# A fused state-space and bilinear feed-forward kernel: decay factors of later blocks by VectorE squares, and another order of the first pairs

## The chip, the cores and the metric

The kernel runs on one core of a Trainium2 chip. The time is device microseconds of one execution, given as the median of several executions. PE is the matrix engine (PEld its weight loads), DVE is VectorE, ACT is ScalarE, POOL is GpSimd and SP only issues transfers.

## The reference

Two layers follow each other. The first is a state-space scan over 768 tokens for 4 batches and 8 heads, the second a bilinear feed-forward layer over the 3072 tokens that come out:

```
for c in range(nc):                                   # chunks of the sequence
    cum = np.cumsum(log_a[chunk])                     # decay within the chunk
    M = (C B^T) * exp(cum_i - cum_j) * causal
    y[chunk] = M x + (C state) * exp(cum)
    state = exp(sum la) * state + sum_j B_j x_j exp(cum_last - cum_j)
x = y.transpose(0, 2, 1, 3).reshape(3072, 256)
out = ((x @ w_a) * (x @ w_b)) @ w_out                 # d_ff = 1536
```

Inputs and outputs are float32; the result of the chunked scan does not depend on the length of a chunk.

## The kernel before

**Blocks and pairs.** The kernel takes chunks of Q = 128 tokens, so there are NBLK = 6 blocks. A pair is two batches of one block; with NBP = 2 pairs a block there are 12 pairs, 0 to 11. Pairs 0 to 3 (p < P0, blocks 0 and 1) hold their tokens split by parity r (token 2i + r on partition i of a half); pairs 4 to 11 (blocks 2 to 5) hold one token a partition, and their B and C are turned by a DMA.

**Decay factors.** `scan` makes running products Pr[bh, block, q] of the decays, one row for each of the 32 (batch, head); `over_mid` makes rmid = 1 / Pr at the middle of each block. The factor of C is Pr times rmid, wanted with tokens on partitions: `factors_mm` gets it by a matmul of Pr with selr, a selection matrix scaled by rmid (`sel_over_mid`), and `factors` copies the result from PSUM into fC on ScalarE. fB is the reciprocal of fC (`fb`). Block 0 is done first, blocks 1 to 5 together.

**A pair's way.** `scale_bc` multiplies B and C with their factors, `transposes` turns them on PE and copies them to SBUF (B once for each parity of the head, through a column of the mask `par`, with the other heads set to zero; C once), `scores` makes C B^T of all heads in four PSUM banks SC[0..3], `mask` multiplies by the causal mask (on VectorE, or by a ScalarE copy and a GpSimd product with `by_pool`), `scale_x` makes the half-precision x, `pv` makes the output of the scan and the sums for the state, and copies the output into X2T (for pair 0 `pv_u` and `evac0` do so by halves of the channels).

**The feed-forward layer.** For pairs 0 to 3 a unit is `unit_mm` with Wa, `unit_mm` with Wb (four 256-column matmuls each, into one bank), a ScalarE copy of the first (`evac_a`) and a VectorE product (`times`). Then follow the matmuls with Wo (`out_mm`, `out_half`). For blocks 2 to 5 `bunit` and `bout` do the same for the four batches at once.

**Order.** The schedule is written out by hand: the order of the calls is the order of the instructions on each engine, and semaphores come from the data. Four PSUM banks are given out in turn by the string BANKS, one digit for each call of `bank`. Loads go by the queues of SP, ACT and POOL; the weights and the first loads of pairs 1 and 2 go by POOL, in order, behind POOL's own work. PE is filled with products of a zero tile (`warmup`) until the first weights are there.

The stretch that the change touches, as it is before, in the order of the calls: the four transposes of pair 1, two units with Wa, `scores(1)`, the third Wa unit, the factors of blocks 1 to 5, pair 1's masks, three Wb units, `pv(1)`, the products for the state factors G (gps), and then the units of pair 1.

Of the kernel before, what the change touches and what calls it, by code (L numbers as in the profile page):

```python
# [18 lines left out]
XS = 1024.0  # L19
YS = 16.0  # L20

BANKS = (
    "0123102310231012301230123012031230123013201320130213021302130213021320312031203102132013"
    "2013203102310231023103210321032103210321032103210231023102310231023102310231023102310231"
)


# [1 line left out]
def kernel(  # L29
# [13 lines left out]
    nc = tc.nc  # L43
# [52 lines left out]
    planes = [big.tile([128, 6, H * N], f16, name=f"planes{t}") for t in range(2)]  # L96
    causal_q = big.tile([128, Q], f16, name="causal_q")
    Pr = big.tile([BH, NBLK, Q], f32, name="Pr")
    rmid = big.tile([BH, NBLK], f32, name="rmid")
    selr = big.tile([BH, NBLK, 2, NBP * H], f32, name="selr")  # L100
    fB = big.tile([128, NBLK, 2, NBP, H], f32, name="fB")
# [25 lines left out]
    def bank(name):  # L127
        return psf.tile([128, 512], f32, name=name, tag=f"ff{next(banks)}")
# [58 lines left out]
    load1(nc.sync, 1, 0, 0)  # L187
    nc.sync.dma_start(c32, p32_t.ap())
    nc.vector.memset(warm.bitcast(u32), 0)
    nc.vector.memset(zero, 0.0)  # L190
    nc.gpsimd.memset(sel, 1.0)
    nc.gpsimd.affine_select(
# [5 lines left out]
        pattern=[[-H, 2], [-2 * H, NBP], [-1, H]],  # L198
        channel_multiplier=1,
    )  # L200
    nc.gpsimd.memset(ident, 1.0)
    nc.gpsimd.affine_select(
        out=ident, in_=ident, compare_op=ALU.is_equal, fill=0.0, base=0, pattern=[[-1, 128]], channel_multiplier=1
    )
    nc.gpsimd.memset(causal, 1.0)
    for bt in range(2):
        v = causal[64 * bt : 64 * bt + 64]
        nc.gpsimd.affine_select(  # L208
# [23 lines left out]
    def sel_over_mid(lo, hi, eng):  # L232
        eng.tensor_tensor(
            out=selr[:, lo:hi].rearrange("p k t c -> p k (t c)"),
            in0=sel.rearrange("p t b h -> p (t b h)").unsqueeze(1).broadcast_to((BH, hi - lo, 2 * NBP * H)),
            in1=rmid[:, lo:hi].unsqueeze(2).broadcast_to((BH, hi - lo, 2 * NBP * H)),
            op=ALU.mult,
        )

    def factors_mm(lo, hi, fps=None, k0=0):  # L240
        if fps is None:
            fps = bank("fps")
        w = 2 * NBP * H
        F = fps[:, k0 * w : (k0 + hi - lo) * w].rearrange("p (k r c) -> p k r c", k=hi - lo, r=2)
        for k in range(lo, hi):
            if k * NBP >= P0:
                for c0 in (0, 64):
                    nc.tensor.matmul(
                        F[c0 : c0 + 64, k - lo].rearrange("p r c -> p (r c)"),
                        Pr[:, k, c0 : c0 + 64],  # L250
                        selr[:, k].rearrange("p t c -> p (t c)"),
                        start=True,
                        stop=True,
                        skip_group_check=True,
                        tile_position=(0, c0),
                    )
                continue
            for r in range(2):
                for bt in range(2):
                    nc.tensor.matmul(  # L260
                        F[64 * bt : 64 * bt + 64, k - lo, r],
                        Pr[:, k].rearrange("p (i r) -> p r i", r=2)[:, r],
                        selr[:, k, bt],
                        start=True,
                        stop=True,
                        skip_group_check=True,
                        tile_position=(0, 64 * bt),
                    )
        return F.rearrange("p k r c -> p (k r c)")

    def factors(lo, hi, fps):
        factors_mm(lo, hi, fps)
        nc.scalar.copy(flat(fC, lo, hi), fps[:, 0 : (hi - lo) * 2 * NBP * H])

    def flat(f, lo, hi):
        return f[:, lo:hi].rearrange("p k r b h -> p (k r b h)")

# [4 lines left out]
    def scale_x(p, eng):  # L282
# [5 lines left out]
        else:  # L288
            eng.tensor_scalar(xo, xi, XS, None, ALU.mult)  # L289

    def scale_bc(p, which, eng, factor=None):
        blk, bp = divmod(p, NBP)
        name, f = (("bm", fB), ("cm", fC))[which]
        raw = by_token(pair_in[p][which]) if p >= P0 else pair_in[p][which].rearrange("p h r n -> p r h n")
        if p >= P0 and which:
            eng.tensor_tensor(  # L296
                out=planes[p % 2][:, 4:6].rearrange("p t (h n) -> p t h n", n=N),
                in0=raw,
                in1=f[:, blk, :, bp].unsqueeze(3).broadcast_to((128, 2, H, N)),
                op=ALU.mult,  # L300
            )
            return
        m_ = mid.tile([128, 2, H, N], f16, name=name, tag=name)
        eng.tensor_tensor(  # L304
            out=m_,
            in0=raw,
            in1=(f[:, blk, :, bp] if factor is None else factor).unsqueeze(3).broadcast_to((128, 2, H, N)),
            op=ALU.mult,
        )
        st.setdefault(p, {})[name] = m_  # L310
        if p >= P0:
            dst = planes[p % 2][:, 0:4].rearrange("p (t e) (m f n) -> p t e m f n", e=2, f=2, n=N)
            for e in range(2):
                eng.tensor_copy(dst[:, :, e, :, e], m_.rearrange("p t (m f) n -> p t m f n", f=2)[:, :, :, e])

    def transposes(p, ps=None, between=None, apart=False):
        s = st[p]
        if ps is None:
            ps = [SC[0], SC[1]] if apart else None
            on_dve = apart  # L320
        else:
            on_dve = True
        TB, TC = (TT[:, 0:256], TT[:, 256:512]) if ps is None else [t_.bitcast(f16)[:, 0:256] for t_ in ps]
        for T_, src in ((TB, s["bm"]), (TC, s["cm"])):
            for r in range(2):
                nc.tensor.transpose(
                    T_[:, r * 128 : (r + 1) * 128], src[:, r].rearrange("p h n -> p (h n)"), ident
                )
            if between:
                between()  # L330
                between = None
        BT = mid.tile([128, 2, 2, 2, 64], f16, name="bt", tag="bt")
        CT = mid.tile([128, 2, Q], f16, name="ct", tag="ct")
        b_ = []
# [261 lines left out]
    def unit_mm(p, k2, W):  # L596
# [13 lines left out]
                )  # L610
        return ps

    def evac_a(a_ps, on_dve=False):
        asb = ffh.tile([128, 512], f32, name="asb", tag="asb")
        (nc.vector.tensor_copy if on_dve else nc.scalar.copy)(asb, a_ps)  # L615
        return asb
# [123 lines left out]
    warmup(1, SC[3], 128)  # L740
    scale_bc(0, 0, nc.vector)
    scale_bc(0, 1, nc.vector, v.rearrange("p (r b h) -> p r b h", r=2, b=NBP)[:, :, 0])
    tb, tcp = bank("tb"), bank("tc")
    transposes(0, [tb, tcp], lambda: warmup(1, SC[3], 128))
    nc.scalar.copy(flat(fC, 0, 1), v)
    scan(3, 4)
    warmup(1, SC[3])
    warmup(2, SC[3], 128)
    scores(0)
# [14 lines left out]
    pv_u(0, 1, py, True)  # L764
    for bt in range(2):
        evac0(1, bt, (nc.scalar, nc.vector)[bt], py)
    scan(4, 5)
    w1 = load_w(1)
    for bt in range(2):
        load1(nc.gpsimd, 2, 0, bt)  # L770
    warmup(1, tcp, 128)
    transposes(1, apart=True)
    scan(5, NBLK)
    over_mid(1, NBLK)
    sel_over_mid(1, NBLK, nc.vector)
    aps = [unit_mm(0, 0, Wa), unit_mm(0, 1, Wa)]
    asb = [evac_a(aps[0])]
    nc.gpsimd.tensor_tensor(out=hr, in0=Pr[:, 0:NG, Q - 1], in1=rmid[:, 0:NG], op=ALU.mult)
    nc.gpsimd.tensor_tensor(out=hs, in0=hr, in1=Pr[:, 1:NBLK, 63], op=ALU.mult)
    nc.gpsimd.tensor_tensor(  # L780
# [2 lines left out]
        in1=selb.rearrange("p (b g) -> p b g", b=nb),  # L783
        op=ALU.mult,
    )
    scores(1)
    mask(product(1, 3), by_pool=True)
    aps.append(unit_mm(0, 2, Wa))
    asb.append(evac_a(aps[1]))
    asb.append(evac_a(aps[2]))  # L790
    fps = bank("fps")
    factors(1, NBLK, fps)
    scale_x(1, nc.scalar)
    for m in range(3):
        mask(product(1, m))
    bps = [unit_mm(0, k2, Wb) for k2 in range(3)]
    for bt in range(2):
        load1(nc.gpsimd, 2, 1, bt)
    load_wo(0)
# [9 lines left out]
    for c0 in (0, 64):  # L809
# [7 lines left out]
            tile_position=(0, c0),  # L817
        )
    nc.scalar.copy(G.rearrange("p b g -> p (b g)"), gps[:, 0 : nb * NG])
    for k2 in range(1, 3):  # L820
        times(0, k2, bps[k2], asb[k2])
    fb(1)
# [26 lines left out]
    h = unit(1, 5)  # L849
    scores(2)  # L850
    mask(product(2, 3), by_pool=True)
    mask(product(2, 0))
    mask(product(2, 1))
    mask(product(2, 2))
    h()
    scale_x(2, nc.scalar)
    scale_bc(3, 0, nc.gpsimd)
    scale_bc(3, 1, nc.gpsimd)
# [197 lines left out]
```

## Time and profile before

| | |
|---|---|
| median of 3 runs | 123.72 us (122.92 to 124.85) |
| the profiled execution | 122.51 us |
| its span, first to last instruction | 120.8 us |
| PE, DVE, ACT, POOL busy | 115.7, 85.2, 72.1, 62.3 us |
| TensorE clock granted | 0.999 |
| PE matmuls of the units, L601 and L667 | 27.8 and 57.1 us |
| transfers | 13.73 MB, mean 114 GB/s |

The page gives busy time for each engine, the chain of work that ended last, and groups of instructions by line. L601 is the matmul of `unit_mm`, L667 that of `bunit`, L248 and L260 those of `factors_mm`, L373 that of `scores` for the first pairs, L433 and L460 those of `pv_u` and `ds_mm`, L615 the copy of `evac_a`, L287 the ScalarE product of `scale_x`. A matmul of float32 operands appears as two records.

### The profile page before, as it was taken

The page shows a single profiled execution, that of the slowest core. Times are in us where ns is not written, and L with a number is a line of the kernel's source. Part 1 is how long each engine was busy: PE and PEld are TensorE (multiplying, and loading weights), DVE is VectorE, ACT ScalarE, POOL GpSimd, SP SyncE. Part 2 cuts the span into 40 slices and gives each one's busy share as a digit, 9 for nine tenths or more (in the row PEclk, how much of TensorE's full clock was granted, in tenths as well). Part 3 has the DMA queues.
Part 4 walks back from the last instruction along what each step waited for, and adds up shares of the span by engine and source line. Part 5 has one row for each costly group of instructions (what it writes and reads, how often), then busy time and mean ns, then how long its engine had stood idle before and what let it go on. Part 6 is the DMA issues. An engine that isn't in the chain of part 4 may idle for free.

```text
span 120.8 us, 3711 instructions
## 1 busy us (share of the span) xinstructions
PE 115.7 (96%) x1455; PEld 79.4 (66%) x1455; DVE 85.2 (71%) x162; ACT 72.1 (60%) x142; POOL 62.3 (52%) x108
## 2 busy tenths in 40 slices
PE   5889999999999999999999999999999999999990
PEld 2445889888898898644476464766464684555890
DVE  1887888882989898499984999677799445847100
ACT  0466757854965767877668637645646737566220
POOL 7999998972795676299731993138400000000200
PEclk9999999999999999999999999999999999999999
DMA  3999999986969999699998874869501012010032
GB/s 62 171 169 233 173 201 159 215 140 70 100 99 126 128 125 144 111 135 146 71 151 111 173 239 126 91 90 159 180 3 49 0 43 87 0 49 0 20 110 87
DMA packets 66641, 13.73 MB, mean 114 GB/s; under 512 B 61616, under 2 KB 66256, under 8 KB 66624
## 3 DMA queue, kind: packets, MB, share of 16 engines
q1 hardware_dynamic: 62448, 9.40, 50.7%
q0 software_dynamic: 2176, 3.74, 17.0%
q10 hardware_dynamic: 2000, 0.36, 1.6%
q8 instruction: 11, 0.18, 0.7%
q14 instruction: 6, 0.05, 0.1%
HBM read 11.13 MB, written 3.15 MB: 118 GB/s over the span
## 4 chain that ended last, share of the span: by engine, by line
PE 89%; DMA 4%; POOL 3%; issue 0%; ACT 0%; POOLq 0%
PE ops L694 18%; PE aps L667 18%; PE bps L667 17%; PE ops L637 9%; PE aps L601 9%; PE bps L601 9%; DMA Wa<-in_moe_w_a_dram 4%; PE SC L358 2%; PE SC L419 2%; POOL cn L148 1%; PE SC L373 1%; PE SC L433 1%; PE SC L508 1%; POOL bn L148 1%; POOL causal L208 1%; PE SC L460 1%
## 5 line engine op out<-in xcount | busy, mean ns | idle before, releaser
L615 ACT COPY asb<-aps 128x512 f32<-128x512 f32 x72 | 41.8, 586 | 14.1 <-PE aps L667 9.7
L679 DVE TENSOR_TENSOR hkb<-bps,asb 128x512 f16<-128x512 f32 x48 | 32.3, 687 | 12.8 <-ACT asb L615 11.6
L667 PE MATMUL aps<-XB,Wa 128*128 128x512 f16 x96 | 28.6, 379 | 0.0
L667 PE MATMUL bps<-XB,Wb 128*128 128x512 f16 x96 | 28.5, 379 | 0.0
L694 PE MATMUL ops<-Wo,hkb 128*128 128x256 f16 (+1 forms) x204 | 22.5, 267 | 0.0
L694 PEld LDWEIGHTS <-hkb 128*128 128x128 f16 x204 | 18.5, 98 | 3.1
L413 DVE TENSOR_TENSOR t<-SC,causal_q 128x512 f16<-128x512 f32 x27 | 17.1, 681 | 3.3 <-PE SC L358 3.3
L622 DVE TENSOR_TENSOR hk<-bps,asb 128x512 f16<-128x512 f32 x24 | 16.2, 685 | 2.4 <-ACT asb L615 1.2
L667 PEld LDWEIGHTS <-Wb 128*128 128x128 f16 x96 | 9.9, 103 | 10.9
L667 PEld LDWEIGHTS <-Wa 128*128 128x128 f16 x96 | 9.7, 103 | 9.1 <-issue 0.2
L708 POOL DMA_DIRECT2D out_dram<-osb x1 | 0.6, 639 | 27.3 <-ACT osb L706 27.3
L706 ACT ACTIVATE osb<-ops 128x256 f32<-128x256 f32 (+1 forms) x16 | 6.0, 376 | 14.3 <-PE ops L694 14.2
L601 PE MATMUL aps<-X2T,Wa 128*128 128x256 f16 x96 | 14.0, 273 | 0.1
L601 PE MATMUL bps<-X2T,Wb 128*128 128x256 f16 x96 | 13.8, 273 | 0.0
L637 PE MATMUL ops<-Wo,hk 128*128 128x256 f16 x96 | 11.5, 273 | 0.0
L601 PEld LDWEIGHTS <-Wa 128*128 128x128 f16 x96 | 9.5, 104 | 1.1 <-DMA Wa<-in_moe_w_a_dram 0.3
L601 PEld LDWEIGHTS <-Wb 128*128 128x128 f16 x96 | 9.8, 103 | 0.6
L411 POOL TENSOR_TENSOR t<-tmp,causal_q 128x512 f16<-128x512 f32 x5 | 5.8, 1159 | 8.0 <-ACT tmp L410 7.9
L637 PEld LDWEIGHTS <-hk 128*128 128x128 f16 x96 | 8.9, 98 | 1.4
L304 POOL TENSOR_TENSOR bm<-bn,fB 128x256 f16<-128x256 f32 x11 | 7.1, 641 | 4.8 <-DMA bn<-in_B_dram 3.6
L289 POOL TENSOR_SCALAR x<-xn 128x512 f16<-128x512 f32 x6 | 8.9, 1489 | 1.0 <-DMA xn<-in_x_dram 0.7
L296 POOL TENSOR_TENSOR planes<-cn,fC 128x256 f16<-128x256 f32 x8 | 5.0, 621 | 7.9 <-DMA cn<-in_C_dram 7.8
(95 smaller groups left out, 124.0 us busy)
## 6 DMA issues: line engine op xcount, KB each, us to landing
out_dram<-osb SPq DMA_DIRECT2D x22, 128.0 KB, 1.8
xn<-in_x_dram SPq DMA_DIRECT2D x7, 256.0 KB, 4.3
cn<-in_C_dram SPq DMA_DIRECT2D x8, 128.0 KB, 4.1
bn<-in_B_dram SPq DMA_DIRECT2D x8, 128.0 KB, 4.6
Wa<-in_moe_w_a_dram POOLq DMA_DIRECT2D x2, 384.0 KB, 5.9
Wb<-in_moe_w_b_dram POOLq DMA_DIRECT2D x2, 384.0 KB, 7.3
Wo<-in_moe_w_out_dram POOLq DMA_DIRECT2D x2, 384.0 KB, 7.2
xn<-in_x_dram POOLq DMA_DIRECT2D x4, 128.0 KB, 7.2
```

Of the source, the lines that this page charges most:

```text
L289: eng.tensor_scalar(xo, xi, XS, None, ALU.mult)
L304: eng.tensor_tensor(out=m_, in0=raw, in1=(f[:, blk, :, bp] if factor is None else factor).unsqueeze(3).broadcast_to((128, 2, H, N)), op=AL ...
L411: nc.gpsimd.tensor_tensor(out=o_, in0=tmp, in1=c_, op=ALU.mult)
L413: nc.vector.tensor_tensor(out=o_, in0=i_, in1=c_, op=ALU.mult)
L601: nc.tensor.matmul(ps[:, kk * 2 * Q : (kk + 1) * 2 * Q], W[k // 6][:, f, k % 6 // 3 * 384 : (k % 6 // 3 + 1) * 384].rearrange("p (c kk) -> ...
L615: (nc.vector.tensor_copy if on_dve else nc.scalar.copy)(asb, a_ps)
L622: nc.vector.tensor_tensor(out=s["hk"][:, 2 * k2 : 2 * k2 + 2, :].rearrange("p k q -> p (k q)"), in0=b_ps, in1=asb, op=ALU.mult)
L637: nc.tensor.matmul(o_ps[:, 0:d_model], hk[:, k, bt * Q : (bt + 1) * Q], Wo[:, k, :], start=(k == 0), stop=(k == NK - 1), skip_group_check= ...
L667: nc.tensor.matmul(t_, W[k // 6][:, f, k % 6 // 3 * 384 : (k % 6 // 3 + 1) * 384].rearrange("p (c kk) -> p kk c", kk=3)[:, k % 3], XB[:, b ...
L679: return lambda: nc.vector.tensor_tensor(out=s["hk"][:, k], in0=ps[1], in1=asb, op=ALU.mult)
L694: nc.tensor.matmul(o_ps[:, 0:w], hk[:, k, c * Q : (c + 1) * Q], Wo[:, k, cs], start=(k == 0), stop=(k == NK - 1), skip_group_check=True,)
L706: nc.scalar.activation(out=o_sb[:, 0:w], in_=o_ps[:, 0:w], func=AF.Copy, scale=1.0 / (YS * YS))
```

## The change

It has several parts, all but the last two in the first 16 us.

- The memsets of `ident` and `causal` go from GpSimd to VectorE.
- The scans of blocks 3 and 4 are called earlier, between the steps of pair 0.
- The first two Wa units of pair 0 are issued together (`units_mm`), first the two units' matmuls with channel half 0, then those with half 1.
- Pair 1's B is copied by one VectorE product with both parities (`joint`), its C by ScalarE.
- selr and the factor matmuls are made for block 1 alone.
- `scores(1)` and the mask product on GpSimd are called ahead of the three GpSimd products for hsx.
- Pair 1's x is scaled in two halves, by ScalarE (heads 0 to 3) and VectorE (heads 4 to 7), behind the masks.
- The third Wb unit of pair 0 is called behind gps instead of ahead of `pv(1)`.
- The factors of blocks 2 to 5 are made later, in pair 2's stretch: ScalarE multiplies Pr by rmid (`over_mid_late`), and VectorE transposes the result in squares of 32 x 32 (`turn_late`). They lie in fC in another order (`of_pair`).
- BANKS is another string.

```diff
+    Prm = big.tile([BH, NBLK, Q], f32, name="Prm")
...
     nc.vector.memset(warm.bitcast(u32), 0)
+    nc.vector.memset(ident, 1.0)
+    nc.vector.memset(causal, 1.0)
     nc.vector.memset(zero, 0.0)
...
-    nc.gpsimd.memset(ident, 1.0)
...
-    nc.gpsimd.memset(causal, 1.0)
...
         for k in range(lo, hi):
-            if k * NBP >= P0:
-                for c0 in (0, 64):
-                    nc.tensor.matmul(
...
-                continue
...
+    def over_mid_late(lo, hi):
+        for k in range(lo, hi):
+            nc.scalar.mul(Prm[:, k], Pr[:, k], rmid[:, k : k + 1])
+
+    def turn_late(lo, hi):
+        for c0 in range(0, Q, BH):
+            nc.vector.transpose(flat(fC, lo, hi)[c0 : c0 + BH].rearrange("p (k c) -> p k c", c=BH), Prm[:, lo:hi, c0 : c0 + BH])
+
+    def of_pair(f, blk, bp):
+        if blk * NBP >= P0:
+            return flat(f, blk, blk + 1).rearrange("p (b r h) -> p b r h", b=NBP, r=2)[:, bp]
+        return f[:, blk, :, bp]
...
+    def scale_x_split(p):
+        X16 = mid.tile([128, H, 2, D], f16, name="x16", tag="x16")
+        xi = pair_in[p][2]
+        st.setdefault(p, {})["X16"] = X16
+        for u in range(2):
+            o_, i_ = [t_[:, 4 * u : 4 * u + 4].rearrange("p h r d -> p (h r d)") for t_ in (X16, xi)]
+            if u:
+                nc.vector.tensor_scalar(o_, i_, XS, None, ALU.mult)
+            else:
+                nc.scalar.mul(o_, i_, XS)
...
+        if joint:
+            b_ = nc.vector.tensor_tensor(
+                out=BT.rearrange("p e r t i -> p e (r t i)"),
+                in0=TB.unsqueeze(1).broadcast_to((128, 2, 256)),
+                in1=par.unsqueeze(2).broadcast_to((128, 2, 256)),
+                op=ALU.mult,
+            )
+            c_ = nc.scalar.copy(
+                CT.rearrange("p t (i r) -> p r (t i)", r=2), TC.rearrange("p (r c) -> p r c", r=2)
+            )
...
+    def units_mm(p, ks, W, order):
+        pss = {k2: bank("aps" if W is Wa else "bps") for k2 in ks}
+        for k2, f in order:
+            for kk in range(2):
...
     scale_bc(0, 1, nc.vector, v.rearrange("p (r b h) -> p r b h", r=2, b=NBP)[:, :, 0])
+    scan(3, 4)
     tb, tcp = bank("tb"), bank("tc")
     transposes(0, [tb, tcp], lambda: warmup(1, SC[3], 128))
     nc.scalar.copy(flat(fC, 0, 1), v)
-    scan(3, 4)
+    scan(4, 5)
...
-    scan(4, 5)
...
-    transposes(1, apart=True)
+    transposes(1, apart=True, joint=True)
     scan(5, NBLK)
     over_mid(1, NBLK)
-    sel_over_mid(1, NBLK, nc.vector)
-    aps = [unit_mm(0, 0, Wa), unit_mm(0, 1, Wa)]
+    sel_over_mid(1, 2, nc.vector)
+    aps = units_mm(0, range(2), Wa, ((0, 0), (1, 0), (0, 1), (1, 1)))
     asb = [evac_a(aps[0])]
+    scores(1)
+    mask(product(1, 3), by_pool=True)
     nc.gpsimd.tensor_tensor(out=hr, in0=Pr[:, 0:NG, Q - 1], in1=rmid[:, 0:NG], op=ALU.mult)
...
-    scores(1)
-    mask(product(1, 3), by_pool=True)
...
-    factors(1, NBLK, fps)
-    scale_x(1, nc.scalar)
+    factors(1, 2, fps)
     for m in range(3):
         mask(product(1, m))
-    bps = [unit_mm(0, k2, Wb) for k2 in range(3)]
+    scale_x_split(1)
+    bps = [unit_mm(0, k2, Wb) for k2 in range(2)]
...
     nc.scalar.copy(G.rearrange("p b g -> p (b g)"), gps[:, 0 : nb * NG])
+    bps.append(unit_mm(0, 2, Wb))
...
     mask(product(2, 3), by_pool=True)
+    over_mid_late(2, NBLK)
     mask(product(2, 0))
     mask(product(2, 1))
     mask(product(2, 2))
     h()
+    turn_late(2, NBLK)
     scale_x(2, nc.scalar)
```

More of the change, by code (lines that the diff above doesn't have):

```diff
@@ L22 @@
 BANKS = (
-    "0123102310231012301230123012031230123013201320130213021302130213021320312031203102132013"
-    "2013203102310231023103210321032103210321032103210231023102310231023102310231023102310231"
+    "0123102310231032103210321032013210231021302130210321032103210321032130123012301203213021"
+    "3021301203120312031201320132013201320132013201320312031203120312031203120312031203120312"
 )
@@ L245, in factors_mm @@
         for k in range(lo, hi):
-            if k * NBP >= P0:
-                for c0 in (0, 64):
[L248 to L256, printed above, removed]
-                continue
             for r in range(2):
@@ L298, in scale_bc @@
                 in0=raw,
-                in1=f[:, blk, :, bp].unsqueeze(3).broadcast_to((128, 2, H, N)),
+                in1=of_pair(f, blk, bp).unsqueeze(3).broadcast_to((128, 2, H, N)),
                 op=ALU.mult,
@@ L306, in scale_bc @@
             in0=raw,
-            in1=(f[:, blk, :, bp] if factor is None else factor).unsqueeze(3).broadcast_to((128, 2, H, N)),
+            in1=(of_pair(f, blk, bp) if factor is None else factor).unsqueeze(3).broadcast_to((128, 2, H, N)),
             op=ALU.mult,
@@ L314, in scale_bc, with transposes @@
                 eng.tensor_copy(dst[:, :, e, :, e], m_.rearrange("p t (m f) n -> p t m f n", f=2)[:, :, :, e])
-    def transposes(p, ps=None, between=None, apart=False):
+    def transposes(p, ps=None, between=None, apart=False, joint=False):
         s = st[p]
@@ L333, in transposes @@
         CT = mid.tile([128, 2, Q], f16, name="ct", tag="ct")
+        if joint:
[8 more added lines that the diff above has]
+            )
+            tc.declare_no_dep(c_.ins, b_.ins.name, reason="reads of two banks")
+            s["BT"], s["CT"] = BT, CT
+            return
         b_ = []
@@ L611, in unit_mm @@
         return ps
+    def units_mm(p, ks, W, order):
+        pss = {k2: bank("aps" if W is Wa else "bps") for k2 in ks}
+        for k2, f in order:
+            for kk in range(2):
+                k = 2 * k2 + kk
+                nc.tensor.matmul(
+                    pss[k2][:, kk * 2 * Q : (kk + 1) * 2 * Q],
+                    W[k // 6][:, f, k % 6 // 3 * 384 : (k % 6 // 3 + 1) * 384].rearrange("p (c kk) -> p kk c", kk=3)[
+                        :, k % 3
+                    ],
+                    X2T[:, p, :, f],
+                    start=(f == 0 and kk == 0),
+                    stop=(f == 1),
+                    skip_group_check=True,
+                )
+        return [pss[k2] for k2 in ks]
     def evac_a(a_ps, on_dve=False):
```

## The prediction

> **What bounds the kernel now.** I read the page first: PE is busy for 96% of the span and holds 89% of the chain that ended last, with the weights' first load (4%) and POOL (3%) in front. Then the chain itself, for 10 to 17 us:
>
> ```profile
> 5.11 5.43 DMA Wa<-in_moe_w_a_dram
> 10.58 1.06 PE aps L601 x8
> 11.64 0.36 PE SC L373 x32
> 12.00 0.55 PE aps L601 x4
> 12.55 0.34 PE fps L260 x8
> 12.90 0.48 PE fps L248 x16
> 13.38 1.43 PE bps L601 x12
> 14.80 0.35 PE SC L433 x32
> 15.33 0.28 PE SC L460 x24
> 15.62 0.22 PE gps L810 x4
> 15.84 0.55 PE aps L601 x4
> 16.39 0.44 PE bps L601 x4
> ```
>
> Columns are start, length, what. Wa lands at 5.11 + 5.43 = 10.54, and from 10.58 the chain is PE without a break, to 118 us. Three kinds of saving are possible: an earlier 10.58, less PE work behind it, and neither counts if PE then waits for something else. A unit of four 256-wide matmuls is 0.44 here, 0.55 when it follows small ones. I compare the end of the first unit after gps: 15.84 + 0.55 = 16.39 us. Everything behind it has the same PE work in both kernels.
>
> What stands ready beside PE is in the timeline (start, length, engine, line, operation, tiles):
>
> ```profile
> 12.13 0.58 ACT L410 COPY tmp<-SC 128x512 f32<-128x512 f32 x1 [0.30 <-PE SC L373]
> 12.61 1.08 ACT L615 COPY asb<-aps 128x512 f32<-128x512 f32 x2
> 13.56 0.33 ACT L273 COPY fC<-fps 128x160 f32<-128x160 f32 x1
> 14.03 0.63 ACT L287 ACTIVATE x<-xn 128x512 f16<-128x512 f32 x1
> ```
>
> ```profile
> 9.17 0.82 POOL L304 TENSOR_TENSOR bm<-bn,fB 128x256 f16<-128x256 f32 x1
> 12.78 0.25 POOL L778 TENSOR_TENSOR hr<-Pr,rmid 32x5 f32<-32x5 f32 x1
> 13.55 1.16 POOL L411 TENSOR_TENSOR t<-tmp,causal 128x512 f16<-128x512 f32 x1
> 7.25 0.74 POOL L148 DMA_DIRECT2D xn<-in_x_dram  x1
> ```
>
> The last row is the issue of the second half of pair 1's x; the DMA view of that window gives it 6.7 us to landing, so 13.95. ACT scales x at 14.03, right behind the landing, ends at 14.66, and PE uses it at 14.80. So the x of pair 1 is only 0.1 us from being the bound already.
>
> **The change, part by part.**
>
> Memsets. On POOL ident's takes 0.20 and causal's 0.31. On VectorE a memset of 256 elements takes 0.27 (warm) and one of 128 0.17 (zero), so ident is ready at 1.19 + 0.17 = 1.36 and causal at 1.63; VectorE's next work waits for a_sb until 3.07, which hides this. POOL selects ident 1.37 to 1.66 and causal 1.66 to 2.47 (0.29, 2 x 0.40) and issues its first load at 2.49 instead of 2.88: 0.39 earlier, and so the seven loads behind it (cn twice, Wa, Wb, xn twice; bn first). Bounds on the landings: 0 (transfers already limit) and 0.39 (issue limits). In the view by windows the DMA share is 0.86, 0.94, 0.74, 0.91, 0.92, 0.89 for 2.5 to 5.5 us, and 1.10 and 1.14 for 8 to 10: against 1.12 some (1.12 - 0.88) / 1.12 x 3.0 = 0.64 us of transfer lay free, enough for 0.39, but shared with SP's and ACT's loads. I take 0.25: Wa 10.29, xn 13.70.
>
> Scans. The fourth and fifth (0.40 each) go into VectorE's idle 5.85 to 6.23 and 6.97 to 7.30; pair 0's C copy moves by 0.04, and the scores still wait for ACT's B (6.74). Cost nothing; uncovered it would be 0.4.
>
> PE's start. Pair 1's bm ends on POOL some 0.13 earlier, since the mask ahead of it waits for tmp (7.87) and no longer for the load issue (7.99). Its four transposes then end at 10.32 (10.45 before). Units start at max(10.29 + 0.04, 10.32) = 10.34, by 0.24 earlier.
>
> Order by channel half. The same eight matmuls. The halves of X2T are ready at 9.44 and 10.25, both ahead of 10.34: nothing gained. The first tile closes with the sixth matmul, so its ACT copy ends at 11.78; ACT's next, tmp, begins at 11.89. Hidden, by 0.1.
>
> B in one product. Two ACT passes (0.84) become one VectorE product of 512 elements: nearest rows 1.89 / 3 = 0.63 (mask) and 0.69 (hk); I take 0.69, bounds 0.63 and 0.84. C goes to ACT (0.43 on VectorE, 0.42 a pass on ACT). B is ready at 11.04, scores can start at 10.34 + 1.06 = 11.40: no wait. VectorE's stretch up to the masks was 10.50 to 11.78, 1.28; now 1.28 - 0.43 + 0.69 - 0.13 (the smaller selr) = 1.41, to 11.76. Masks begin 0.13 after the scores' end, 11.89: covered by 0.13.
>
> Factors. 0.48 of PE goes, and ACT's fC copy falls from 0.33 to 0.18 (the 128x32 copy). PE reaches pair 1's pv at 10.34 + 1.06 + 0.36 + 0.55 + 0.34 + (1.43 - 0.44) = 13.64, because the third Wb unit is put behind gps. Before, it was 14.80.
>
> What pv then waits for. ACT: tmp from 11.89, asb twice, fC: 11.89 + 0.58 + 1.08 + 0.18 = 13.73, just after the landing at 13.70. Half of x: SBUF 512 takes 0.63; PSUM rows of 512 and 256 give 0.59 and 0.38, so the half saves 0.20 and takes 0.43 (bounds 0.32, exactly half, and 0.43). It ends at 14.18, and PE follows 0.07 later as before: 14.25. VectorE: masks 11.89 to 13.78, its half 0.29 to 0.42 (the 128x128 and 128x256 X2T rows), to 14.20 at most, which the second half of pv needs at 14.43. So **PE stands from 13.64 to 14.25, 0.61**, where before it never stood. ScalarE's fixed price speaks against splitting: the Trainium skill's page "VectorE: DVE Perf Modes", section on the TRN2 errata, gives ScalarE 224 cycles plus one per element from SBUF, by an estimate 0.61 for 512 (row: 0.63, agreeing) and 0.40 for 256; with that the sum below would be 0.03 better.
>
> The sum: from 14.25, pv 0.35, state sums 0.46, gps 0.22, the moved unit 0.55, the first unit of pair 1 0.44 = 2.02, so 16.27 against 16.39: **0.1 us gained**. Of 0.24 (start) + 0.48 (factors) = 0.72, the stall takes 0.61 back.
>
> POOL's order. Its mask now comes first: loads end at 12.67, mask to 13.83, hr to hsx 0.80, to 14.63; gps needs it at 15.07. Hidden by 0.44.
>
> Banks. I followed each of the four banks through pair 3; the tile before is read at least 0.1 us before the next is written, so nothing. One missed costs a copy, 0.59.
>
> Late factors. Four ACT products of 32x128: between 0.28 (128x128 row) and 0.42, in all 1.1 to 1.7, from 25.12 where ACT has 1.10 idle; x of pair 2 ends 0 to 0.6 later, by 27.4, and pv needs it at 27.93. Four VectorE squares, which no row shows: between 0.17 (128-element memset) and 0.69 (512-element product), nearest 0.40 (32x128 scan), so 1.6 of the 1.64 that VectorE is idle there:
>
> ```profile
> 26.27 0.68 DVE L622 TENSOR_TENSOR hk<-bps,asb 128x512 f16<-128x512 f32 x1
> 28.59 0.42 DVE L493 TENSOR_SCALAR X2T<-SC 128x256 f16<-128x256 f32 x1 [1.64 <-PE SC L460]
> ```
>
> Cost nothing, at 0.69 each 2.76 - 1.64 = 1.1. The same page, section on the three transpose paths, has 311 ns for such a turn of 128x128 in bf16; by it the four would be 1.24, hidden; no run yet shows it. First use is POOL's cn of pair 4 at 30.14.
>
> **Against the runs.** The profiled execution took 122.51 (span 120.8 and 1.7 around it); less 0.1 it is 122.4. The median shown, 123.72, lies 1.2 above it, so I give 123.6 for a median. The three runs spread 122.92 to 124.85.
>
> **Rivals.**
>
> Forecast, x of pair 1 takes over as the bound: 123.6, own range 123.5 to 123.8. Chance 0.50.
>
> A, the loads come no earlier, transfers being saturated (share over 1 from 5.5 on speaks for it; the free 0.64 before it against). Units at 10.58, xn at 13.95, half of x 14.01 to 14.44, pv 14.51, the mark at 16.53: +0.14, 123.9. Chance 0.15.
>
> B, little stall: x is ready and pv waits only for the masks (13.78 + 0.06 = 13.84), the mark at 15.86: -0.5, 123.2. It needs x 0.4 sooner than the largest shift of the issue allows with ACT's chain as it is. Chance 0.10.
>
> C, slower: VectorE's half of x waits for POOL. In the row of 9.17 above POOL's bm takes 0.82, beside VectorE's cm (9.10 to 9.51), and 0.62 elsewhere: they hinder each other by 0.2. If the half, coming at 13.78, must wait for POOL's mask and hr to hsx (14.63), it ends at 15.05 and pv's second half starts 0.68 late: +0.6, 124.3. It decides from a start later than 13.95. The skill's "SBUF — State Buffer", section on who interferes with whom, says that one of the two blocks for a whole instruction; with the 0.82 row the trace agrees in sign. Between instructions VectorE can get in, so chance 0.15.
>
> D, the squares cost 0.7 or more: X2T of pair 2 is late by 1.1, 124.7; over 1.0 each it is 2.4 or more, 126. Chance 0.10, of it 0.05 for the upper end.
>
> That the factor matmuls stay is excluded by the code; only those of block 1 are left.
>
> **The numbers.** What a measurement can tell from no change is about 2%, 2.5 us. Only the top of D reaches it, and 0.03 of C with POOL's loads held up too: slower 0.08. No case gains 2.5; 0.04 is left for the spread of the medians. Within: 0.88. Range: from B less 0.8 of spread, 122.4, to D, 125.0.
>
> **What would show it.** Right: no L248 rows; Wa landing near 10.3; in the chain an ACT x or a DMA xn piece of some 0.6 just ahead of SC L433; the unit after gps ending near 16.3; ACT and VectorE rows at 25 to 28.6 with PE unbroken. Wrong: pv at 13.9 (B), a late DVE x row (C), a gap at 28.6 (D), or any PE gap behind 17 us.

## The result, and the profile after

The changed kernel takes 123.55 us, the median of 22 runs (122.94 to 124.57); the kernel before, in the same comparison, 123.3 us. The ratio is 1.0042 with a 95% interval of 1.0026 to 1.0059: slower by some 0.5 us, far inside the 2% named in the prediction, but with the sign opposite to the 0.1 us forecast. All ratios here leave out the slow executions of either kernel, so this one is not the quotient of the two medians, which lie only 0.25 us apart.

The profiled execution of after has a span of 122.2 us, 1.4 more than before's. This is its chain of waits (start, length, what), from POOL's sixth load to the first unit of pair 1:

```profile
6.22 0.66 POOL xn L149
6.88 8.14 DMA xn<-in_x_dram
...
15.11 0.42 ACT x L302
...
15.57 0.42 PE SC L459 x32
15.99 0.30 PE SC L486 x32
16.30 0.22 PE gps L853 x4
16.52 0.55 PE bps L627 x4
17.07 0.44 PE aps L627 x4
```

The line numbers have moved: L459 is pv (L433 before), L486 the state sums (L460), L853 gps (L810), L627 the units (L601). Before, the chain was PE from 10.58 on. Now it leaves PE at pv and runs through ScalarE's half of x into the load of x, as the prediction said it would: x has become the bound. But x landed at 15.02, not at 13.70. The point that the prediction followed, the end of pair 1's first unit, is 17.07 + 0.44 = 17.51, against 16.39 before and 16.27 forecast.

The same stretch in the timeline (start, length, engine, line, operation, tiles, and in brackets the engine's idle time ahead of the row and what ended it):

```profile
2.50 0.88 POOL L149 DMA_DIRECT2D bn<-in_B_dram  x1
5.77 0.42 DVE L317 TENSOR_TENSOR cm<-cn,fps 128x256 f16<-128x256 f32 x1 [0.17 <-DMA cn<-in_C_dram]
11.23 0.78 PEld L644 LDWEIGHTS <-Wa 128*128 128x128 f16 x8 [0.62 <-DMA Wa<-in_moe_w_a_dram]
15.12 0.35 DVE L300 TENSOR_SCALAR x<-xn 128x256 f16<-128x256 f32 x1 [0.43 <-DMA xn<-in_x_dram]
15.57 0.42 PE L459 MATMUL SC<-t,x 64*32 64x128 f16 x32 [1.02 <-ACT x L302]
```

POOL's first load is issued at 2.50, against 2.88 before, as worked out. Yet the first Wa matmul comes at 11.23 instead of 10.58, and VectorE waits for pair 0's C, which it did not do before. PE stands 1.02 us for x. The account of the 1.12 us at the first unit: units start 0.65 later; from there to pv 4.34 instead of 4.22 (0.48 of factors and 0.44 of a unit fewer, the 1.02 more); and from pv to the end of the unit 1.94 instead of 1.59, since the moved unit now lies there. The rest of the 1.4 is a second wait, far behind. Up to 77 us the chain of after runs 1.12 to 1.13 behind that of before (the same group of Wo matmuls at 77.69 and 76.56), and from the next such group on 1.35 (81.39 and 80.04). In between, PE waits for ScalarE's copy `osb`, which it does not do before:

```profile
79.98 0.05 issue
80.03 0.39 ACT osb L749
80.42 0.04 issue
80.46 0.59 PE bps L710 x2
```

By BANKS, this second `bps` tile lies in both kernels in the bank that `osb` empties, so the bank's order is not the difference. ScalarE comes late to `osb`, because its copies to XB have waited 0.48 for VectorE's state products U. VectorE starts these after 0.56 us of idle time instead of 0.18; the row names PE's state sums, but they had ended by 77.7, so why it starts late stays open:

```profile
76.74 0.97 DVE L565 SCALAR_TENSOR_TENSOR U<-SC,G,gU 128x64 f32<-128x64 f32 x4 [0.18 <-PE SC L447]
78.24 0.86 DVE L591 SCALAR_TENSOR_TENSOR U<-SC,G,gU 128x64 f32<-128x64 f32 x4 [0.56 <-PE SC L473]
```

One execution is not the median. The same kernel profiled again (r1 below) had a span of 121.1, 0.3 more than before's, with x at 13.76 and PE's stall at 0.37. Its first unit ends only 0.08 later than before's, and the other 0.22 is the same wait for `osb`, at 78.98. None of the other eighteen traces has a wait at that place. What differed between the two traces of the changed kernel was above all when the loads landed.

### The profile page after: what moved, and what is told of

Read it like the earlier page. It is cut to its first block, busy times and chain, and to the rows that moved or that the text cites. A ratio compares the mean times of both kernels' runs of the same rounds, so it can differ in the third digit from the quotient of the medians.

```text
span 122.2 us, 3688 instructions
## 1 busy us (share of the span) xinstructions
PE 115.8 (95%) x1439; PEld 79.1 (65%) x1439; DVE 87.6 (72%) x169; ACT 72.6 (59%) x145; POOL 62.0 (51%) x106
## 2 busy tenths in 40 slices
DMA packets 66641, 13.73 MB, mean 112 GB/s; under 512 B 61616, under 2 KB 66256, under 8 KB 66624
## 3 DMA queue, kind: packets, MB, share of 16 engines
HBM read 11.13 MB, written 3.15 MB: 117 GB/s over the span
## 4 chain that ended last, share of the span: by engine, by line
PE 85%; DMA 7%; POOL 4%; ACT 1%; issue 0%; DVE 0%; ACTq 0%
PE ops L737 18%; PE bps L710 17%; PE aps L710 17%; PE ops L680 9%; PE bps L627 8%; PE aps L627 8%; DMA xn<-in_x_dram 7%; PE SC L384 2%; PE SC L445 2%; POOL cn L149 1%; PE SC L459 1%; PE SC L534 1%; POOL bn L149 1%; POOL causal L209 1%; POOL Wa L166 1%; POOL Wb L166 1%
## 5 line engine op out<-in xcount | busy, mean ns | idle before, releaser
L665 DVE TENSOR_TENSOR hk<-bps,asb 128x512 f16<-128x512 f32 x24 | 16.3, 686 | 2.5 <-ACT asb L658 1.3
L710 PEld LDWEIGHTS <-Wa 128*128 128x128 f16 x96 | 9.7, 103 | 9.1 <-issue 0.2
L749 ACT ACTIVATE osb<-ops 128x256 f32<-128x256 f32 (+1 forms) x16 | 6.0, 377 | 14.2 <-PE ops L737 14.1
L627 PE MATMUL bps<-X2T,Wb 128*128 128x256 f16 x96 | 14.0, 273 | 0.0
L627 PE MATMUL aps<-X2T,Wa 128*128 128x256 f16 x88 | 12.9, 273 | 0.0
L627 PEld LDWEIGHTS <-Wb 128*128 128x128 f16 x96 | 9.7, 103 | 0.6
L627 PEld LDWEIGHTS <-Wa 128*128 128x128 f16 x88 | 8.8, 103 | 0.7
```

The costliest lines, as they stand in the source:

```text
L627: nc.tensor.matmul(ps[:, kk * 2 * Q : (kk + 1) * 2 * Q], W[k // 6][:, f, k % 6 // 3 * 384 : (k % 6 // 3 + 1) * 384].rearrange("p (c kk) -> ...
L665: nc.vector.tensor_tensor(out=s["hk"][:, 2 * k2 : 2 * k2 + 2, :].rearrange("p k q -> p (k q)"), in0=b_ps, in1=asb, op=ALU.mult)
L710: nc.tensor.matmul(t_, W[k // 6][:, f, k % 6 // 3 * 384 : (k % 6 // 3 + 1) * 384].rearrange("p (c kk) -> p kk c", kk=3)[:, k % 3], XB[:, b ...
L749: nc.scalar.activation(out=o_sb[:, 0:w], in_=o_ps[:, 0:w], func=AF.Copy, scale=1.0 / (YS * YS))
```

## The experiments

Every ratio is to the kernel before, on the same chip in the same call. Chips differ: the median of before was between 122.93 and 123.89 in five calls, so times of different calls are not compared directly. The intervals are some 0.3% wide on each side, about the size of what is looked for; the traces carry more of the argument than the ratios. They are compared up to the first unit behind gps, since ten of the twenty have PE waits between 35 and 68 us, of 0.05 to 1.6 us each, most of them for the turned B and C of the later blocks, in kernels with and without the change.

**The memsets, and with them the earlier loads.** e1 takes them out of the changed kernel, e2 puts them alone into the kernel before.

```diff
-    nc.vector.memset(ident, 1.0)        # e1; e2 is the reverse, in before
-    nc.vector.memset(causal, 1.0)
+    nc.gpsimd.memset(ident, 1.0)
+    nc.gpsimd.memset(causal, 1.0)
```

> The changed kernel with the two memsets back on GpSimd, all else as changed. Theory 1 (the earlier issue of POOL's loads makes them and pair 0's loads get in each other's way, so everything lands later): pair 0's C lands before 5.1 us again, Wa near 10.5, pair 1's x near 13.9 instead of 15.0; PE stands about 0.6 us ahead of pv instead of 1.0; 0.5 to 1.0 us faster than the changed kernel. Theory 2 (landings vary from one execution to the next, the memsets do nothing): landings anywhere between 10.5 and 11.2 for Wa, the time within 0.15 us of the changed kernel.

> The kernel before with the two memsets on VectorE, nothing else. Theory 1: Wa near 11.2, pair 1's x near 15.0, and with the third Wb unit still ahead of pv a stall of about 0.6 us there; 0.5 to 0.7 us slower than before. Theory 2: within 0.15 us of before, and POOL's first load issued at 2.5 instead of 2.9 us.

e1: 1.0026 (0.9999 to 1.0053). e2: 1.0042 (1.0016 to 1.0068), as much as the whole change. In e2 the loads are issued at 2.50, and the first Wa matmul is at 11.13 (10.37 in e1). To part the memsets from the earlier issue, e7 keeps e2 and lets POOL make two more memsets, on tiles that nobody reads, so that its first load goes out at 2.73:

```diff
+    nc.gpsimd.memset(ident_2, 1.0)
...
+    nc.gpsimd.memset(causal_2, 1.0)
```

> The kernel before with the two memsets on VectorE, as in the run with only the memsets, but GpSimd makes the same two memsets on spare tiles, so that its first load is issued at 2.9 us again. If the earlier issue costs the time: pair 0's C lands at 4.9 again instead of 5.1 to 5.7, the time is that of before within 0.2 us. If VectorE's memsets cost it (its later work or what GpSimd waits for): still 0.4 to 0.5 us slower than before.

e7: 1.0005 (0.997 to 1.0041). Three kernels were then run again on one chip, after as r1, e2 as r2 and e7 as r3:

> The changed kernel again, beside the next three on one chip, for its landings and its time: theory issue (the earlier first load of GpSimd makes pair 0's C land later and the start of PE with it) has C at 5.3 us or later, ratio 1.003 to 1.006; theory chance has C as in the kernels that issue at 2.9 us.

> The kernel before with only the memsets moved, again, on one chip with the next. Theory issue: pair 0's C 0.3 to 0.6 us later than in the next run, ratio to before 1.003 to 1.006. Theory chance: equal to the next within 0.2%.

> The memsets on VectorE with GpSimd's first load at 2.9 us, again, on one chip with the run ahead. Theory issue: ratio to before 0.999 to 1.001, C earlier than in the run ahead. Theory chance: no difference between the two.

r1: 1.0028 (1.0002 to 1.0054). r2: 1.0013 (0.9986 to 1.004). r3: 1.0005 (0.9982 to 1.0029). So the memsets in themselves cost nothing that shows. For the earlier issue the ratios lean one way (1.0042 and 1.0013 against 1.0005 twice) and overlap. The traces, those of the kernels below with the same warm-ups and loads included, lean the same way. In the five with the issue at 2.5 us (after, e2, e3, r1, r2) pair 0's last piece of C landed between 5.43 and 5.80 and the first Wa matmul came between 10.66 and 11.24, 11.0 in the mean. In the nine with the issue at 2.73 to 2.9 (before, e1, e4 to e8, r3, r4) it was 5.01 to 5.42 for C, without overlap, and 10.32 to 11.52, 10.7 in the mean, for the matmul. Pair 0's scores, which PE does first, began at 6.82 to 7.18 in the five and at 6.65 to 6.96 in the nine. The issue view of the first 2.7 us shows whom the early load meets (tiles, queue, count, size, us from issue to landing); first before:

```profile
cn<-in_C_dram SPq DMA_DIRECT2D x1, 32.0 KB, 2.8
cn<-in_C_dram ACTq DMA_DIRECT2D x1, 32.0 KB, 2.8
ch<-ph SPq DMA_DIRECT2D x1, 5.0 KB, 2.5
```

and after:

```profile
bn<-in_B_dram POOLq DMA_DIRECT2D x1, 64.0 KB, 3.8
cn<-in_C_dram SPq DMA_DIRECT2D x1, 32.0 KB, 3.3
cn<-in_C_dram ACTq DMA_DIRECT2D x1, 32.0 KB, 3.5
ch<-ph SPq DMA_DIRECT2D x1, 5.0 KB, 3.3
```

POOL's load of pair 1's B now runs beside the last small loads that pair 0 needs, on the queues of SP and ACT, and these take 0.5 to 0.8 us longer. They are needed first: C by VectorE (the wait of 0.17 in the timeline row of 5.77), ph by ScalarE's copy of B. The Trainium skill's page "DMA: Bandwidth & Descriptors", section "Issuing engines are not separate DMA queues", says that loads from several engines run on the same 16 DMA engines and interleave, so that another issuer saves only issue time; these rows agree, in that a load on one queue goes with longer loads on two others.

**The third Wb unit, and both parts undone.** e3 puts it back ahead of pv in the changed kernel; e6 is e3 and e1 together.

```diff
-    bps = [unit_mm(0, k2, Wb) for k2 in range(2)]
+    bps = [unit_mm(0, k2, Wb) for k2 in range(3)]
...
-    bps.append(unit_mm(0, 2, Wb))       # and BANKS to suit
```

> The changed kernel with the third Wb unit of pair 0 issued ahead of pv(1), as before the change, and the two bank digits swapped with it. If PE stands ahead of pv because pair 1's x is late (any reason), the unit fills 0.44 us of it: 0.4 to 0.5 us faster than the changed kernel, as fast as before or 0.1 faster. If instead pv's own order behind it sets the end (X2T late), no gain.

> The changed kernel with the memsets on GpSimd and the third Wb unit ahead of pv. Theory x: pv near 14.4 with no stall over 0.3 us, the first pair-1 unit ends near 16.0, 0.4 us ahead of the kernel before, ratio 0.9965. Theory fetch: a break in the state-sum matmuls to 15.4, the unit ends near 16.4, ratio 1.000.

e3: 1.0023 (0.9993 to 1.0052). e6: 1.0015 (0.9983 to 1.0048). What the unit's place is worth follows from rows. When x lands late, at L, the changed kernel starts pv at L + 0.55 (landing 15.02, pv 15.57) and ends the first unit 1.94 later: L + 2.49. Before, pv comes at L + 0.77 (e10 below: landing 14.95, pv 15.72), and the unit ends 1.59 later: L + 2.36. The halves of x gain 0.22, and the unit that filled the wait before costs 0.35. With the unit ahead again it is L + 0.55 + 1.65 (e3: pv 14.56, end 16.21) = L + 2.20. By these, an estimate, e6 should beat before by 0.16 where x binds; in its trace pv starts at L + 0.55, as it should, but the unit ends at L + 2.44, for the reason that follows.

**The late factors alone**, in the kernel before:

```diff
+    over_mid_late(2, NBLK)
...
+    turn_late(2, NBLK)                  # and factors(1, 2, fps) for factors(1, NBLK, fps)
```

> The kernel before with only the factors of blocks 2 to 5 made late (ScalarE products, VectorE squares, no factor matmuls for them). If pair 1's x sets pv in the kernel before as well, the 0.48 us of PE turn into a stall ahead of pv and the gain is 0 to 0.1 us. If PE alone bounds it, 0.45 us faster. If the squares are uncovered at 26 to 28.6 us, slower by what they exceed 1.64 us by.

e4: 1.0016 (0.9982 to 1.005). In this execution Wa landed 0.24 later than before's. From the first unit to pv it is 3.84 us instead of 4.22, so most of the 0.48 is gained there, and x, which landed at 13.89, costs PE only 0.04. Yet from pv (14.66) to the end of the unit (16.54) it is 1.88 instead of 1.59: PE stood 0.24 within the state sums, at 15.30.

**A break in the state sums.** e1's chain of waits shows the same break, for nothing that the profile names ("issue"):

```profile
13.91 0.42 ACT x L302
...
14.38 0.42 PE SC L459 x32
14.80 0.26 PE SC L486 x28
15.06 0.40 issue
15.46 0.21 PE SC L486 x4
15.67 0.22 PE gps L853 x4
```

e5 is e1 with x taken away as the bound:

```diff
-        xi = pair_in[p][2]
+        xi = pair_in[0][2]              # scale_x_split: pair 1 uses pair 0's x
```

> The changed kernel with the memsets on GpSimd (as in the run with them back), and pair 1's x scaled from pair 0's x tile, which has long landed: the output is another one, the instructions are the same. Theory x (the landing of pair 1's x alone sets pv): PE stands only for the masks, pv starts near 13.9 instead of 14.4, and the first pair-1 unit ends near 15.9 instead of 16.8: 0.5 to 0.9 us faster than with the memsets back. Theory fetch (PE also waits at its 450th record, in the state-sum matmuls, for a block of its own instructions, which has come 2.8 us after a transfer that starts near 12.6 in every trace): pv starts near 13.9, but the break moves to those matmuls and lasts until 15.4; the unit ends at 16.7, the time within 0.15 us.

e5: 1.0017 (0.999 to 1.0045). Its chain:

```profile
13.86 0.32 ACT x L302
...
14.22 0.47 PE SC L459 x32
14.69 0.24 PE SC L486 x28
14.92 0.53 issue
15.45 0.21 PE SC L486 x4
15.66 0.22 PE gps L853 x4
```

pv starts 0.16 earlier than in e1, the break grows by 0.13, and gps is at 15.66 against 15.67. Something other than x holds PE at that place in its program. Counted over its matmul and weight-load records, PE broke at the 447th or 448th in before, e1, e4, e5, e6, r3 and r4, with pauses of 0.2 or less there in e3, e7 and e8 too, and at the 446th in e10. In before it is the 0.09 here:

```profile
15.15 0.09 PE SC L460 x8
15.24 0.09 issue
15.33 0.28 PE SC L460 x24
```

The trace has beside it a transfer of the queue named "instruction", whose 11 transfers move 0.18 MB, 16 KB each: in these traces it starts at 12.4 to 13.1 us (15.39 in e10), and PE goes on 2.7 to 2.95 us after it starts (2.3 in e10). In the other nine traces PE comes to that record 2.86 to 4.0 us after the start, and shows no such pause. So PE seems to wait for its own next instructions, and these seem to be held up by the same loads as x; no view names the wait. With 36 records more ahead of it the place should move by 18 pairs of matmul and weight load; e8 is e6 with that, run again as r4:

```diff
-    warmup(6, SC[3])
+    warmup(24, SC[3], 128)
```

> As the run with the memsets back and the Wb unit ahead, with the first six 512-column warm-up matmuls cut into 24 of 128 columns: the same PE time, 36 more PE records ahead. Theory fetch: the block boundary and the start of its transfer move 36 records earlier in the program, into the scores and pv of pair 1; no break in the state sums, the first pair-1 unit ends near 16.0, 0.4 us faster than the same without it and 0.3 to 0.4 us faster than before. Theory x: no difference to the same without it, within 0.15 us.

> The version with memsets on GpSimd, the third Wb unit ahead of pv and 36 more PE records in the warm-up, on one chip with the changed kernel. All three causes (issue, order, fetch) are taken away in it: ratio to before 0.997 to 0.999, 0.5 us or more faster than the changed kernel, no break in the state sums. If the landing of pair 1's x is the only bound, 1.000.

e8: 1.0000 (0.9968 to 1.0031), with under 0.1 at that record; here Wa had landed late, at 11.47, and PE came to it late. r4: 1.0009 (0.9983 to 1.0036), and a break of 0.66 between the 6th and 7th state sum, where e6 has it (0.25) between the 24th and 25th: moved by 18, as the count says, but not gone.

Four kernels move it the other way or further. e9 is e6, and e10 is before, with the same twelve warm-up matmuls fewer; e12 is e6 with eighteen fewer; e11 is before with every wide warm-up cut in four, 90 records more.

```diff
-    warmup(6, SC[3])
-    warmup(2, SC[3], 128)
+    warmup(4, SC[3])
...
-    warmup(5, tcp)
+    warmup(3, tcp)                      # e9, e10; and six single ones of 128 columns
```

> The changed kernel with the memsets on GpSimd, the third Wb unit ahead of pv, and 12 warm-up matmuls fewer (all eight of 128 columns, two of the first six, two of the five behind pair 0's masks): 24 PE records fewer ahead. Theory fetch (PE can't pass its 447th record before about 15.4, whatever lies ahead): the 447th record now lies behind gps, no break in the state sums, the first pair-1 unit ends near 16.0, ratio to before 0.996 to 0.998. Theory x alone: as with the warm-ups, 1.000 to 1.0015.

> The kernel before with the same 12 warm-up matmuls left out. Theory fetch: its break in the state sums of 0.09 to 0.18 us goes, at most 0.2 us faster, ratio 0.998 to 1.000. Otherwise 1.000; slower if the granted clock falls without them.

> The kernel before with all its 512-column warm-up matmuls cut into four of 128: the same PE time, 90 PE records more ahead. Theory fetch: the 447th record lies 90 records earlier in the program, among pair 0's Wb units at about 14.1 us, and PE stands there until about 15.4: the first pair-1 unit ends 0.8 to 1.2 us later, ratio 1.006 to 1.010. Theory x alone: 1.000, since PE has the same work.

> As the run with 12 warm-up matmuls fewer, with 18 fewer in all (one left of the first six, none of the five): 36 PE records fewer. Theory fetch: no further gain than with 12 fewer, since x and the masks set pv, unless the clock falls for want of PE work ahead of 10 us, which would show as a granted clock below 1 there and 0.5 us or more lost.

e9: 1.002 (0.9987 to 1.0053), no break, but PE stood 0.51 for x, which landed at 14.49. e10: 1.0127 (1.0074 to 1.018). e11: 1.0087 (1.0053 to 1.0121), as expected from the break, but its trace does not show the break: the transfer starts at 11.69, and PE passes the record at 15.20. Where its time goes stays open. e12: 1.0104 (1.0057 to 1.0151); PE already stood 1.26 ahead of 8.61, and its matmuls then ran at about half the pace up to 14.2 (the eight Wa matmuls from 10.81 took 1.89, 1.05 in e9). In e9 and e10 pair 0's scores took 0.65 instead of 0.43, and the Wa matmuls 1.05 as ever. So leaving warm-ups out also slowed PE for a while, and changes more than the count. e10's chain of waits:

```profile
15.72 0.42 PE SC L433 x32
16.13 0.18 PE SC L460 x19
16.32 1.37 issue
17.69 0.25 PE SC L460 x13
```

Fewer records do move the break, from behind the 8th to behind the 19th state sum, but it became 1.37 long; here the instruction transfer started only at 15.39. What sets that start is open; moving records by warm-ups did not give a kernel without the wait.

**Less to transfer.** If both x and the instructions wait for the weights' transfer, a smaller one should free both. e13 is e6 with only the first half of Wb's first tile loaded and used twice; e14 is before with the same.

```diff
+                        W[0][:, :, 0:384], src.rearrange("(f p) e -> p f e", p=128)[:, :, 0:384]
...
+    def part3(W, k):
+        return 0 if W is Wb and k < 6 else k % 6 // 3 * 384
```

> The version with memsets on GpSimd and the third Wb unit ahead of pv, loading only the first half of Wb's first tile (192 KB less into SBUF ahead of pair 1's x) and using it twice: the output is another one, every engine's instructions are the same in number and size. Theory transfers (what the change saves on PE is eaten by waits for transfers: pair 1's x, and PE's own instruction block): x lands near 12.8, pv starts near 14.1 behind the masks and the Wb units, the first pair-1 unit ends near 15.7 if the instruction block comes earlier too, near 16.3 if it does not; ratio to before 0.994 to 0.996, or 0.999. Rival, the saving was never there (other waits on VectorE, ScalarE, GpSimd): 1.000 to 1.0015, as with the whole tile.

> The kernel before with the same half of Wb's first tile. Theory transfers: PE has work up to 14.8 anyway, so x near 12.8 gains nothing but the break of 0.1 us: ratio to before 0.998 to 1.000. If transfers bound the kernel before by more than that: below 0.998.

e13: 0.9969 (0.9949 to 0.9988), 122.53 us against 123.04. e14: 1.001 (0.9976 to 1.0043). e13's chain:

```profile
12.81 1.54 PE bps L637 x12
14.35 0.41 PE SC L469 x32
14.75 0.28 PE SC L496 x32
...
15.06 0.29 PE gps L863 x4
...
15.38 0.62 PE aps L637 x4
```

x lands at 12.99, the instruction transfer starts at 11.79 and there is no break; the unit ends at 16.00. In e14, with x at 12.98, it ends at 16.42, much as before (16.39). So the removed PE work shows as soon as x and the instructions are not late: of the 0.42 between the two ends, 0.38 is the shorter way from the first unit to pv (3.83 against 4.21) and 0.14 an earlier start of the units in that execution, less 0.10 behind pv. Which of the two, x or the instructions, held it back is not parted by this, and the intervals of the two ratios touch. e13 leaves out work that the layer needs and is no version to use. Of those that compute everything, none beat the kernel before; e8 comes nearest, at 1.0000 and 1.0009.

## Why the prediction was right or wrong

**Right: what would bind.** The factor matmuls of blocks 2 to 5 are gone, and the pieces of x stand in the chain right ahead of pv. In r1, where the loads landed almost as forecast (Wa 10.39, x 13.76), the chain of waits has the working almost term by term:

```profile
12.77 0.98 ACT asb L658 x2
...
13.84 0.43 ACT x L302
...
14.31 0.58 PE SC L459 x32
14.88 0.28 PE SC L486 x32
```

ScalarE's half at 13.84 (forecast 13.73), 0.43 long (0.43), pv at 14.31 (14.25), the unit's end at 16.47 (16.27). The last difference of 0.20 is 0.06 at pv's start, 0.05 in pv and state sums (0.86 for 0.81) and 0.09 at gps (15.17 to 15.48, 0.31 for 0.22).

**Wrong: the landings.** The step that failed is "I take 0.25: Wa 10.29, xn 13.70", with its bounds "0 ... and 0.39". The issue did come 0.38 earlier. The landings did not follow: over the five traces with the early issue and the nine with the later one, the median landing of Wa is 10.71 against 10.61, that of x 13.83 against 13.94. Where Wa did land early, in r1 at 10.39, the first matmul still came only at 10.66 (10.34 forecast); pair 0's scores, ahead of it on PE, had slipped to 7.11 from before's 6.73. So rival A, saturated transfers, was the nearer case, and it too had no change of the landings as its worst end. What could make the earlier issue a loss was not in the sum: the loads of SP and ACT that POOL's earlier one runs beside took 0.5 to 0.8 us longer, and PE's start hangs on them. The prediction saw that the 0.64 us of free transfer were "shared with SP's and ACT's loads" and gave it no price. That this loss is there in the median is likely, not shown: the ratios overlap.

**Wrong: nothing behind the first unit.** The prediction followed the sum to 16.3 us and took the rest as equal, since, in its words, "Everything behind it has the same PE work in both kernels"; its banks were followed through pair 3. It named "any PE gap behind 17 us" as a sign of being wrong, and there is one: the wait for `osb` at 80 us, 0.23 in after and 0.22 in r1. In r1 that is most of the 0.30 between the spans. The PE work is the same there, and the bank comes free later. The wait is in both traces of the changed kernel; how often it comes in the other executions is not known.

**Missing: the break in the state sums.** The sum put everything behind pv at fixed PE times, 2.02. With PE work removed ahead of it, PE can come early to its 447th record, and then it stops, it seems for its instructions; it stood 0.18 to 0.66 there in e1, e4, e5, e6, r3 and r4. In other traces, after and r1 among them, it came there later and did not wait, so this does not explain the time of those two; it stands where parts of the change were undone (0.40 in e1, 0.25 in e6). The prediction named two limits on the saving, x and the masks; this was a third, at its longest worth more than the term that was saved (0.48). It is already in the kernel before, as the 0.09 of "issue" at 15.24. The prediction's first fence leaves out this row and the one ahead of it, the text calls the chain PE "without a break", and the 0.46 for the state sums holds the 0.09.

**Mis-sized: the moved unit.** The sum charged 0.55 for it and set no value against what it had covered. Where x binds it is worth 0.35, more than the 0.22 that the halves of x gain. By the prediction's own rows, the unit left in its place would have fitted into the stall of 0.61.

**Most of the smaller terms held.** ScalarE's and VectorE's halves of x took 0.417 and 0.353 in after (0.43; 0.29 to 0.42), the joint product of B 0.692 (0.69). The late factors are hidden as foreseen; in the groups by form (count, busy us, mean ns, idle before):

```profile
L266 ACT ACTIVATE Prm<-Pr,rmid 32x128 f32<-32x128 f32 x4 | 1.3, 388 | 0.0
L270 DVE STREAM_TRANSPOSE fC<-Prm 32x128 f32<-32x128 f32 x4 | 1.2, 299 | 0.0
L348 DVE TENSOR_TENSOR bt<-SC,ch 128x512 f16<-128x512 f16 x1 | 0.7, 692 | 0.2 <-PE SC L339 0.2
L302 ACT ACTIVATE x<-xn 128x256 f16<-128x256 f32 x1 | 0.4, 417 | 0.7 <-DMA xn<-in_x_dram 0.7
```

A square took 0.30, not 0.40, so rival D is out. Rival C is there, but small. In after, VectorE's half began at 15.12, when POOL's mask was done, and doesn't test it. In r1 it ran from 14.02 beside POOL's mask (13.15 to 14.36) and took 0.51, in e3 and e13 0.52; it did not wait for POOL's hr to hsx, and pv took 0.58 instead of 0.42. That is under 0.2, not C's 0.6. Rival B needed x earlier than it came; e13, where it did come earlier but the unit lies ahead of pv, ends at 16.00 against B's 15.86.

What stays open: how the 0.5 us divide among the parts. Undoing the earlier issue and the unit's place together (e6, e8, r4: 1.0015, 1.0000, 1.0009) takes most of the loss away, and each alone (1.0026, 1.0023) part of it, but the intervals do not part these numbers. Nor is it known why VectorE's U comes late at 78 us in the changed kernel alone.

## What to carry to other kernels

PE work removed ahead of a load that is just in time is worth little until the load comes earlier, and where transfers are nearly saturated an earlier issue on one queue can delay the loads on the others: look up what is in flight at the new issue time, and who needs that first. A unit that fills a wait should be moved only when the wait is gone. A small "issue" piece in the middle of one line's matmuls, at the same place in several traces, is a bound like any other, and removing work ahead of it makes it longer. Compare two traces to their end, mark by mark: where the distance between the same rows changes, a wait lies between, even if both kernels have the same code there.

## What the runs showed that was not expected

A wait of TensorE that looks like one for its own instructions. Where it broke off, it was at the 447th or 448th record (once the 446th), and it went on 2.3 to 2.95 us after a 16 KB transfer of the instruction queue had begun; the longest was 1.37 us. With half a Wb tile less to load the transfer began at 11.79 and 11.86 (e13, e14), earlier than in any trace with the whole tile but e11's, and no wait was left. In e10, with twelve warm-up matmuls fewer, it began at 15.39, for a reason that these runs do not show; that kernel was 1.3% slower.

And a wait of 0.22 us at 80 us, in a stretch whose code the change does not touch, in both traces of the changed kernel and in no other.
